# Batch 0 of a fused attention and feed-forward kernel: low parts of q and k of two head pairs, and the fourth pair's planes, on other engines

## The chip, the cores and the metric

The kernel runs on one core of a Trainium2 chip. The metric is the device time of one execution in microseconds; the median of the runs is compared. The engines are TensorE (PE, with its weight loads as PEld), VectorE (DVE), ScalarE (ACT), GpSimd (POOL) and SyncE (SP), which here only issues DMAs. Each engine works through its own queue in order and waits on semaphores that the others raise.

## The reference

Two parts follow each other. The first is attention over 8 batches of 8 heads, with 512 local and 32 global tokens of 64 dimensions; local queries see the global tokens and a window of 32 to each side. The second is a feed-forward part on the result, with a gate by a cosine.

```python
k_all = concat([k_g, k_l]); v_all = concat([v_g, v_l])
out_g = softmax(scale * q_g @ k_all.T) @ v_all
s_ll = where(abs(pos_q - pos_k) <= 32, scale * q_l @ k_l.T, -1e9)
s_lg = scale * q_l @ k_g.T
out_l = softmax(concat([s_lg, s_ll])) @ v_all
x = concat([out_g, out_l]) -> [4352 tokens, 512]
h = x @ w_in            # 512 -> 2048
out = (h * cos(h)) @ w_out   # 2048 -> 512
```

## The kernel before

**Precision.** The matmuls run on f16 operands. To keep float32 accuracy, each operand is first scaled by a power of two and split into a high part (its f16 rounding) and a low part (the rest, again f16). Three products high·high, high·low and low·high are summed in PSUM. So each value passes two steps: something writes the high part (a cast or a scaled copy), and a subtraction writes the low part. These splits are the bulk of the work of ACT, DVE and POOL.

**Attention, by pairs.** Heads are worked on in pairs, four to a batch; p is the pair, b the batch.
- `load_qk` (L452) loads q and k of a pair. For batch 0 the pairs 1 to 3 go into parts of the tile `wo_l`, which is not yet used for weights; the profile therefore calls them `wo_l`.
- `qk_a` to `qk_c` (L489 to L519) find the scale. `qk_a` needs the absolute sum from ACT (L495).
- `qk_d` (L521) makes the high part `qa` and the low part `kl`, 2 x 608 = 1216 columns. The list `QE0` (L76) gives the way for each pair of batch 0. 1: ACT scales in place (L237 in `scaled`), ACT casts (L533), POOL subtracts in four pieces of 304 columns (L231 in `pool_tt`). 2: the same, but POOL does the scaling (L240). 4: ACT scales and casts in one instruction (L537), DVE subtracts in one instruction that scales too (L538). Batch 1 on uses the last way.
- `qk_e` (L543) moves halves between partitions: two copies to `kh` (L547, L548), one from `kl` to the upper half of `qa` (L550), then one within `kl` (L552). For pair 0 of batch 0 some of them are made by DVE, otherwise by SP's DMAs. Each waits for the one whose source it overwrites.
- `sc_a`, `sc_b`, `sc_c` (L600 to L640) do scores (PE), mask and minimum (DVE, L623), and Exp (ACT, L446). A pair has four windows i of 192, 224, 224 and 192 columns, and two heads in each.
- `sc_d` (L672) normalizes the exponentials by the reciprocals `sm` and splits them into `planes`. The list `PLS` (L69) gives the way for each window in batch 0. 3: POOL multiplies (two instructions, L685), ACT casts (L693), POOL subtracts (two, L695). 4: ACT multiplies (L688), then the same cast and subtractions. 1: ACT writes the high part scaled (two, L702), DVE subtracts (two, L705). 2: as 1, but DVE writes the high part too (L704).
- `sc_e` (L707) transposes the planes; in batch 0 by PE (L714) with copies out of PSUM by ACT or DVE (L715).
- `av_a`, `av_b` (L729 to L778) multiply with v and write x, again as high and low part. `g_a` to `g_g` do the same for the global queries, once in two pairs.

**Weights.** W_in is decoded from 64-bit words in eight pieces (`w_in_piece`, L343): ACT scales (L237), DVE puts the bits together (L263, L266, L268), ACT casts the high part `wi_h` (L281), POOL subtracts `wi_l` (L231, four instructions of 256 columns). W_out is first read for its maxima (L407, DVE L288), then loaded again and decoded in 16 pieces during the first slots of the chunk loop; two of these loads, L244, use buffers that the W_in pieces hold before.

**Feed-forward.** The 4096 local tokens form 16 chunks of 256; a last one holds the 256 global tokens. A chunk has eight slots; in each, `m1_a` (L919) does 24 matmuls of W_in, then come range reduction and sine (L941, L942, L446), the gate (L954 to L961), and, three slots later, `m2_a` (L975 to L977) with W_out. Each chunk of batch 0 needs all four pairs of batch 0.

**Order.** The body lists each step with a slot and a phase (`at`), from slot -24 to the end; slots below 0 are the head. For batch 0, pair p starts at slot -21 + p and its steps follow at fixed distances (`tight`). Slot and phase give a priority. A planner with a timeline of its own then puts the instructions on the engines' queues: it takes the ready instruction with the best priority, by its own costs. So the order on a queue can change wherever an instruction moves to another engine.

Of the kernel before, what the change touches and what calls it, by code (L numbers as in the profile page):

```python
# [49 lines left out]
PL = 1  # L50
# [10 lines left out]
PL0 = 0  # L61
PL1 = 3
# [3 lines left out]
GFB = 3  # L66
GFW = 3
UW = 1
PLS = [3, 4, 3, 4]  # L69
DEFN = [0, 0]  # L70
TPE = [1, 1, 1, 1]
TPV = [1, 0, 1, 0]
WLV = 0
HIE = [1, 1, 1, 1]
SHV = [1, 0, 0, 0]
QE0 = [1, 4, 2, 1]  # L76
DI = 3
LVK = -1
LQK = -1
# [58 lines left out]
def body(tc, qk, v, wi, wo, mask, out):  # L138
# [5 lines left out]
    with ExitStack() as ctx:  # L144
# [376 lines left out]
        def qk_d(b, p):  # L521
# [6 lines left out]
            else:  # L528
                kl = ap_.tile([P, 2, NZ], F16, tag="kl", name=f"kl_{nm}")
            qe = QE[min(b, 2)] if b else QE0[p]  # L530
            if qe < 3:
# [110 lines left out]
        def sc_r(b, p):  # L642
            rr = st["sm", b, p]
            if b < 2 and DEFN[b]:
                nc.vector.tensor_scalar(rr, rr, 1e-9 * 2.0**14, 2.0**-22, op0=ALU.add, op1=ALU.mult)
                nc.vector.reciprocal(rr, rr)
                rh = ap_.tile([P, 8], F16, tag="rh", name=f"rh_{b}_{p}")
                rl = ap_.tile([P, 8], F16, tag="rl", name=f"rl_{b}_{p}")
                nc.vector.tensor_copy(rh, rr)
                nc.vector.tensor_tensor(rl, rr, rh, op=ALU.subtract)  # L650

                pr = ps.tile(
                    [P, SL], F32, tag="att" if b else "po", name=f"pr_{b}_{p}", bufs=3 if b else 2
                )
                for i in range(4):
                    for k, part in enumerate((rh, rl)):
                        for h in range(2):
                            r = part[:, 2 * i + h : 2 * i + h + 1]
                            r = bass.AP(tensor=r.tensor, offset=r.offset, ap=[r.ap[0], (0, D)])
                            nc.tensor.matmul(  # L660
                                pr[64 * h : 64 * h + 64, i * P : (i + 1) * P], r, ident16,
                                start=(i == 0 and k == 0), stop=(i == 3 and k == 1),
                                skip_group_check=True,
                            )
                sr = w1.tile([P, SL], F32, tag="sr", name=f"sr_{b}_{p}", bufs=1)
                nc.scalar.copy(sr, pr)
                st["sr", b, p] = sr
                return
            nc.vector.tensor_scalar(rr, rr, 1e-9, 2.0**-10, op0=ALU.add, op1=ALU.mult)
            nc.vector.reciprocal(rr, rr)  # L670

        def sc_d(b, p, i):  # L672
            if i == 0:
                sc_r(b, p)
            t, rr = st.pop(("t", b, p, i))[0], st["sm", b, p]
            w = WIN[i][1]
            pl = PLS[i] if b == 0 else (PL0, PL1, PL)[min(b, 2)]
            if b < 2 and DEFN[b]:
                pl = 5
            if pl in (0, 3, 4, 5):  # L680
                if pl == 3:
                    r = rr[:, 2 * i : 2 * i + 2]
                    rb = bass.AP(tensor=r.tensor, offset=r.offset, ap=[r.ap[0], (1, 2), (0, w)])
                    for h in range(2):
                        nc.gpsimd.tensor_tensor(t[:, h], t[:, h], rb[:, h], op=ALU.mult)  # L685
                if pl == 4:
                    for h in range(2):
                        nc.scalar.activation(t[:, h], t[:, h], AF.Copy, scale=rr[:, 2 * i + h : 2 * i + h + 1])  # L688
                for h in range(2 if pl == 0 else 0):
                    nc.vector.tensor_scalar(t[:, h], t[:, h], rr[:, 2 * i + h : 2 * i + h + 1], None, op0=ALU.mult)  # L690
                hi = planes[i][:, :, 0, OFF[i] : OFF[i] + w]
                lo = planes[i][:, :, 1, OFF[i] : OFF[i] + w]
                (nc.scalar.copy if pl != 5 or HIE[i] else nc.vector.tensor_copy)(hi, t)  # L693
                for h in range(2):
                    nc.gpsimd.tensor_tensor(lo[:, h], t[:, h], hi[:, h], op=ALU.subtract)  # L695
            else:
                for h in range(2):
                    hi = planes[i][:, h, 0, OFF[i] : OFF[i] + w]
                    lo = planes[i][:, h, 1, OFF[i] : OFF[i] + w]
                    r = rr[:, 2 * i + h : 2 * i + h + 1]  # L700
                    if pl == 1:
                        nc.scalar.activation(hi, t[:, h], AF.Identity, scale=r)  # L702
                    else:
                        nc.vector.tensor_scalar(hi, t[:, h], r, None, op0=ALU.mult)  # L704
                    nc.vector.scalar_tensor_tensor(lo, t[:, h], r, hi, op0=ALU.mult, op1=ALU.subtract)  # L705
# [308 lines left out]
        def attn_pair(b, p, o):  # L1014
# [11 lines left out]
            for i in range(4):  # L1026
                at(o["sc"][i], PA, sc_a, b, p, i)
                at(o["sc"][i], PA if o["tight"] else PC, sc_b, b, p, i)
                at(o["ex"], PI, sc_c, b, p, i)
                at(o["sd"], PF, sc_d, b, p, i)  # L1030
                at(o["tr"][i], PA2, sc_e, b, p, i)
# [177 lines left out]
```

## Time and profile before

| | us |
|---|---|
| median of 3 runs | 1044.99 (1041.33 to 1047.4) |
| profiled execution, device time | 1047.05 |
| its span, first to last instruction | 1045.2 |
| busy in the span: PE, DVE, ACT, POOL | 891.6, 705.4, 720.4, 475.4 |
| mean granted TensorE clock | 0.957 |

A table of stretches gives, for each, its start and end, its length, the busy time of PE, PEld, DVE, ACT and POOL with the number of instructions, the granted clock, the DMA share and GB/s. A timeline lists instructions by start and duration in us; in square brackets stands the idle time before an instruction and who ended it. Neighbouring instructions of one kind are merged (x4). The chain of waits goes back from the last instruction of a stretch, at each step to what released it. A group row has busy us, mean ns, and idle time before.

### The profile page before, as it was taken

What the parts mean: (1) busy time and instruction counts of PE and PEld (TensorE: products, weight loads), DVE (VectorE), ACT (ScalarE), POOL (GpSimd) and SP (SyncE); (2) the same over time, 40 slices, a digit from 0 to 9 for tenths busy, and PEclk for the clock granted to TensorE, in tenths of its full rate; (3) what the DMA queues carried; (4) which work ended last, traced back from release to release, by engine and by line L of the source; (5) the groups of instructions that cost most, each with busy time, mean ns of one, the idle gap of its engine ahead of it and who ended that gap; (6) DMA issues with size and microseconds to landing.
All of it is one profiled execution on the core that took longest, in us unless ns stands there. A gap on an engine that the chain in (4) does not pass through costs nothing.

```text
span 1045.2 us, 21138 instructions
## 1 busy us (share of the span) xinstructions
PE 891.6 (85%) x7947; PEld 608.2 (58%) x7947; DVE 705.4 (67%) x1801; ACT 720.4 (69%) x1470; POOL 475.4 (45%) x513
## 2 busy tenths in 40 slices
PE   1344677678999998999899988999889999999996
PEld 0232554454566665666666655666656676666663
DVE  5996588887468777777778677777777776433231
ACT  5786788887477776877687777867777777444342
POOL 3698477886333332433243423333334333444442
PEclk9995898887999999999999999999999999999998
DMA  9786025867254546353554455355545452200000
GB/s 371 274 299 222 14 69 147 201 150 159 93 109 92 117 90 146 86 114 89 152 100 117 95 147 106 94 104 141 107 104 102 109 89 57 48 21 21 1 21 21
DMA packets 165823, 120.20 MB, mean 115 GB/s; under 512 B 143064, under 2 KB 143064, under 8 KB 163672
## 3 DMA queue, kind: packets, MB, share of 16 engines
q1 hardware_dynamic: 165720, 118.85, 45.2%
q8 instruction: 62, 1.02, 0.4%
q14 instruction: 41, 0.34, 0.1%
HBM read 56.00 MB, written 8.91 MB: 62 GB/s over the span
## 4 chain that ended last, share of the span: by engine, by line
PE 36%; DVE 22%; ACT 15%; DMA 13%; POOL 7%; issue 5%; SPq 1%; ACTq 0%; DVEq 0%; POOLq 0%
PE ph L919 15%; DMA qkr<-qk 7%; PE po L975 6%; PE po L977 5%; PE po L976 5%; DVE planes L705 4%; DVE t L623 3%; DMA vr<-v 3%; ACT planes L702 3%; ACT L446 3%; DVE u L942 3%; ACT t L446 2%; POOL planes L695 2%; PE acc L750 2%; DVE kl L538 2%
## 5 line engine op out<-in xcount | busy, mean ns | idle before, releaser
L919 PE MATMUL ph<-xh,wi_h 128*128 128x256 f16 x1024 | 282.8, 277 | 17.1 <-DVE gf L956 15.2
L919 PE MATMUL ph<-xl,wi_h 128*128 128x256 f16 x1024 | 283.1, 277 | 0.0
L919 PE MATMUL ph<-xh,wi_l 128*128 128x256 f16 x1024 | 282.9, 276 | 0.0
L961 POOL TENSOR_TENSOR gl<-gf,gh 128x512 f16<-128x512 f32 x136 | 167.3, 1234 | 236.7 <-ACT gh L960 236.6
L954 POOL TENSOR_TENSOR w<-w 128x512 f32<-128x512 f32 x136 | 142.4, 1051 | 268.8 <-ACT w L446 268.8
L919 PEld LDWEIGHTS <-wi_h 128*128 128x128 f16 x2176 | 212.2, 99 | 60.7 <-issue 18.6
L975 PE MATMUL po<-wo_h,gh 128*128 128x512 f16 x544 | 206.5, 384 | 29.1 <-DVE o L983 17.9
L976 PE MATMUL po<-wo_l,gh 128*128 128x512 f16 x544 | 208.2, 383 | 7.3 <-POOL wo_l L231 7.2
L977 PE MATMUL po<-wo_h,gl 128*128 128x512 f16 x544 | 207.8, 383 | 0.0
L446 ACT ACTIVATE w<-u,ca 128x512 f32<-128x512 f32 x136 | 97.7, 721 | 109.5 <-DVE u L942 107.6
L942 DVE SCALAR_TENSOR_TENSOR u<-u,cm,ph 128x512 f32<-128x512 f32 x136 | 100.8, 741 | 97.4 <-ACT u L941 97.4
L446 ACT ACTIVATE t<-t,mn 128x192 f32<-128x192 f32 (+1 forms) x256 | 116.9, 458 | 49.7 <-DVE mn L623 49.1
L956 DVE SCALAR_TENSOR_TENSOR gf<-w,ph 128x512 f32<-128x512 f32 x136 | 92.6, 681 | 56.3 <-POOL w L954 56.1
L960 ACT CAST gh<-gf 128x512 f16<-128x512 f32 x136 | 83.1, 611 | 68.3 <-DVE gf L956 59.5
L919 PEld LDWEIGHTS <-wi_l 128*128 128x128 f16 x1088 | 107.9, 99 | 15.1 <-issue 1.2
L941 ACT ACTIVATE u<-ph,cm 128x512 f32<-128x512 f32 x136 | 92.2, 679 | 21.5 <-PE ph L919 20.0
L623 DVE CUSTOM_DVE_ANT_0 t<-ps,msk,al 128x192 f32<-128x192 f32 (+1 forms) x256 | 99.2, 425 | 11.3 <-PE ps L607 11.1
L977 PEld LDWEIGHTS <-gl 128*128 128x128 f16 x544 | 53.6, 99 | 71.7 <-issue 9.9
L976 PEld LDWEIGHTS <-gh 128*128 128x128 f16 x544 | 53.5, 98 | 70.1 <-issue 21.8
L705 DVE SCALAR_TENSOR_TENSOR planes<-t,sm,planes 128x192 f16<-128x192 f32 (+1 forms) x192 | 83.9, 486 | 10.5 <-ACT planes L702 10.4
L975 PEld LDWEIGHTS <-gh 128*128 128x128 f16 x544 | 53.2, 98 | 62.3 <-issue 13.9
L446 ACT ACT_TABLE_LOAD x57 | 73.1, 1283 | 1.0
(188 smaller groups left out, 1435.7 us busy)
## 6 DMA issues: line engine op xcount, KB each, us to landing
qkr<-qk SPq DMA_DIRECT2D x29, 608.0 KB, 4.4
vr<-v SPq DMA_DIRECT2D x8, 1280.0 KB, 8.4
kh<-qa SPq DMA_DIRECT2D x62, 152.0 KB, 2.6
out<-o SPq DMA_DIRECT2D x34, 256.0 KB, 3.1
raw_wm<-wo SPq DMA_DIRECT2D x16, 512.0 KB, 6.5
qa<-kl SPq DMA_DIRECT2D x31, 152.0 KB, 3.4
kl<-kl SPq DMA_DIRECT2D x31, 152.0 KB, 3.6
wo_h<-wi SPq DMA_DIRECT2D x4, 1024.0 KB, 9.1
```

The lines of the kernel that those rows point to most:

```text
L446: ins = nc.scalar.activation(*a, **k).ins
L623: nc.vector.tensor_tensor_reduce(t[:, h], pt[:, h], msk[:, MOFF[i] : MOFF[i] + w], al, 3.0e38, ALU.add, ALU.min, mn[:, h : h + 1],)
L705: nc.vector.scalar_tensor_tensor(lo, t[:, h], r, hi, op0=ALU.mult, op1=ALU.subtract)
L919: nc.tensor.matmul(ph[:, a], w[:, kc, f], x[:, kc, q], start=first and ip == 0, stop=last and ip == 2, skip_group_check=True,)
L941: nc.scalar.activation(u, ph, AF.Identity, bias=m)
L942: nc.vector.scalar_tensor_tensor(u, u, m, ph, op0=ALU.subtract, op1=ALU.subtract)
L954: nc.gpsimd.tensor_tensor(w, w, w, op=ALU.mult)
L956: nc.vector.scalar_tensor_tensor(gf, w, 0.5, st.pop(("ph", c, j)).rearrange("p a b -> p (a b)"), op0=ALU.subtract, op1=ALU.mult,)
L961: nc.gpsimd.tensor_tensor(gl, gf, gh, op=ALU.subtract)
L975: nc.tensor.matmul(po[k], gh[:, q], wo_h[:, f], start=(f == 0), stop=False)
L976: nc.tensor.matmul(po[k], gh[:, q], wo_l[:, f], start=False, stop=False)
L977: nc.tensor.matmul(po[k], gl[:, q], wo_h[:, f], start=False, stop=(f == NJ - 1))
```

## The change

Two lists are changed and one line reads them.
- `QE0`: pairs 2 and 3 of batch 0 go from ways 2 and 1 to way 4.
- `PLS` gets a row for each pair. Pairs 0 to 2 keep ways 3, 4, 3, 4 for the four windows. Pair 3 gets 1, 2, 1, 4: windows 0 and 2 by ACT (high part) and DVE (low part), window 1 by DVE alone, window 3 as before.

```diff
-PLS = [3, 4, 3, 4]
+PLS = [[3, 4, 3, 4], [3, 4, 3, 4], [3, 4, 3, 4], [1, 2, 1, 4]]
...
-QE0 = [1, 4, 2, 1]
+QE0 = [1, 4, 4, 4]
...
-            pl = PLS[i] if b == 0 else (PL0, PL1, PL)[min(b, 2)]
+            pl = PLS[p][i] if b == 0 else (PL0, PL1, PL)[min(b, 2)]
```

## The prediction

> **What bounds the kernel now.** I read the table of stretches first, since the edit touches only batch 0. PE, PEld, DVE, ACT and POOL busy, granted clock, DMA share and GB/s for each stretch:
>
> ```profile
> 0.00:60.00 60.00, 13.18 (x85) 8.87 (x85) 46.91 (x135) 40.88 (x83) 34.42 (x52) 1.00 0.85 322
> 60.00:122.00 62.00, 32.84 (x380) 23.87 (x381) 40.85 (x117) 42.66 (x87) 47.27 (x70) 0.75 0.54 180
> 122.00:190.00 68.00, 51.62 (x424) 36.74 (x422) 53.62 (x135) 60.86 (x115) 49.34 (x67) 0.90 0.41 110
> 190.00:260.00 70.00, 51.34 (x523) 33.40 (x523) 59.11 (x158) 55.50 (x117) 53.45 (x70) 0.83 0.75 166
> 260.00:500.00 240.00, 230.49 (x2060) 156.19 (x2058) 169.01 (x437) 169.98 (x354) 88.17 (x77) 0.99 0.48 107
> ```
>
> From 260 us on PE is busy 96% of the time (230.49 of 240). Before 122 us it is busy 46.0 of 122 us: this is the head, in which batch 0 is prepared and PE waits for other engines. Only here can the edit gain. Cutting the head finer shows who holds it:
>
> ```profile
> 48.80:75.00 26.20, 10.92 (x100) 8.08 (x98) 25.86 (x59) 20.10 (x28) 26.15 (x30) 1.00 0.89 295
> 75.00:91.50 16.50, 4.44 (x62) 3.19 (x59) 16.15 (x54) 12.73 (x31) 16.50 (x25) 0.72 0.98 360
> 91.50:101.00 9.50, 6.50 (x63) 5.12 (x65) 1.39 (x3) 4.04 (x6) 9.22 (x16) 0.50 0.23 74
> ```
>
> Three things are full at once from 48.8 to 91.5 us: POOL (42.65 of 42.7 us), DVE (42.01) and, from 75 us, the DMA engines (0.98). After 91.5 us only POOL stays full (9.22 of 9.5) while DVE falls to 1.39: POOL is the last to finish. The chain of waits, followed back from the end of the head (start, duration, what), says the same:
>
> ```profile
> 48.85 4.53 POOL wi_l L231 x4
> 55.51 2.57 POOL t L685 x4
> 64.34 6.66 POOL planes L695 x7
> 74.68 9.75 DMA kh<-qa
> 88.31 3.05 POOL t L685 x4
> 91.35 3.21 POOL planes L695 x6
> 94.56 2.52 POOL wi_l L231 x4
> 97.11 0.33 SPq L244
> 97.53 4.23 DMA kl<-kl
> ```
>
> The last steps matter most. SP's queue holds a load of raw W_out (L244) until POOL has finished wi_l at 97.08, because the buffer is still in use. Behind it stands the copy kl<-kl of the fourth pair (97.53), and that pair's scores cannot start until it lands at 101.76. So the fourth pair, and with it the first full chunk of the feed-forward part, starts when POOL's queue has run to that wi_l.
>
> **The change part by part.** POOL's timeline has the work that goes:
>
> ```profile
> 53.34 2.21 POOL L240 TENSOR_TENSOR wo_l<-wo_l,qs 128x1216 f32<-128x1216 f32 x1
> 61.42 2.93 POOL L231 TENSOR_TENSOR kl<-wo_l,qa 128x304 f16<-128x304 f32 x4
> 79.26 3.09 POOL L231 TENSOR_TENSOR kl<-wo_l,qa 128x304 f16<-128x304 f32 x4
> 108.88 2.01 POOL L685 TENSOR_TENSOR t<-t,sm 128x192 f32<-128x192 f32 x4 [8.15 <-DVE sm L670]
> 111.57 4.54 POOL L695 TENSOR_TENSOR planes<-t,planes 128x192 f16<-128x192 f32 x8 [0.69 <-ACT planes L693]
> ```
>
> *Edit A, q and k of the third and fourth pair.* POOL loses 2.21 + 2.93 + 3.09 = 8.23 us, all ahead of the wi_l that releases L244. ACT: for the third pair a cast becomes a scaled activation; for the fourth, one of two activations goes. DVE gains two subtractions of 1216 columns. What those cost and how such an operation acts on POOL is in these rows (group summary: min/median/max ns):
>
> ```profile
> L538 DVE SCALAR_TENSOR_TENSOR kl<-qkr,qs,qa x28: 1466/1696/2345, 141.1 to 835.8; 128x1216 f16<-128x1216 f32 x28
> L231 POOL TENSOR_TENSOR wi_l<-y_wi,wi_h x32: 664/670/1698, 40.4 to 100.0; 128x256 f16<-128x256 f32 x32
> 51.63 1.22 DVE L268 SCALAR_TENSOR_TENSOR y_wi<-y_wi,lo_wi 128x1024 uint32<-128x1024 uint32 x1
> 51.68 1.70 POOL L231 TENSOR_TENSOR wi_l<-y_wi,wi_h 128x256 f16<-128x256 f32 x1
> ```
>
> The same POOL subtraction takes 0.67 us normally and 1.70 us when it starts just behind a DVE operation with two inputs in SBUF: it lost 1.03 us to an operation of 1.22 us, 0.84 of its length. The two new DVE operations are of this kind. At 1.70 us each (the median, since POOL is busy beside them), DVE gains 3.4 us; POOL loses 0.84 x 1.47 = 1.2 us to each, 2.5 in all (the undisturbed length, as the extra is DVE waiting for POOL). So POOL's queue gets shorter by 8.23 - 2.5 = 5.7 us.
>
> The Trainium skill, "SBUF — State Buffer", section "Who interferes with whom", says that a DVE instruction with two SBUF inputs and a GpSimd instruction that reads SBUF exclude each other, so that the loser waits for the whole instruction. By that rule edit A would be worth a little less, an estimated 5.3 us, and moving work between these two engines pays only by the difference of their speeds; the row above agrees with the exclusion and puts the loss at 1.03 of 1.22 us.
>
> The bounds of A. Upper: no blocking, 8.2 us. Lower: DVE, itself full, holds the queue. The DVE step that feeds the decisive wi_l is this one:
>
> ```profile
> 86.48 1.34 DVE L268 SCALAR_TENSOR_TENSOR y_wi<-y_wi,lo_wi 128x1024 uint32<-128x1024 uint32 x1
> 89.91 1.04 ACT L281 CAST wi_h<-y_wi 128x1024 f16<-128x1024 f32 x1
> 94.53 2.55 POOL L231 TENSOR_TENSOR wi_l<-y_wi,wi_h 128x256 f16<-128x256 f32 x4
> ```
>
> With DVE's order unchanged and 3.4 us more in front, it ends at 91.2; plus 1.04 for the cast and 2.55 for POOL that is 94.8, against 97.08 now: 2.3 us gained. In between is the likeliest, nearer POOL's side, because 10.6 us of DVE's work in this stretch are the maxima of W_out, needed only after the scores of batch 0, and the planner may put these behind:
>
> ```profile
> L288 DVE TENSOR_REDUCE wos<-raw_wm 128x1 f32<-128x512 f32 x16 | 10.6, 673 | 0.0
> ```
>
> I take 5.7.
>
> *Edit B, planes of the fourth pair.* POOL loses 10 operations after 108.88: four multiplications (2.01 us) and six of eight subtractions; it now ends at 116.11. ACT loses the multiplications and cast of the second window and the casts of the first and third, and gets four scaled activations instead. DVE gets two scaled copies and six subtractions. Batch 2 on does this, and its rows price the subtraction and the activation; a scaled copy by DVE (L704) appears nowhere, so I bound it between the 0.2 us of the reciprocal on 8 columns and the 0.478 us of the subtraction, and take the latter, the same width:
>
> ```profile
> L705 DVE SCALAR_TENSOR_TENSOR planes<-t,sm,planes 128x192 f16<-128x192 f32 (+1 forms) x64 | 27.6, 478 | 3.0 <-ACT planes L702 3.0
> L702 ACT ACTIVATE planes<-t,sm 128x192 f16<-128x192 f32 (+1 forms) x64 | 24.3, 452 | 0.0
> 108.53 0.20 DVE L670 RECIPROCAL sm<-sm 128x8 f32<-128x8 f32 x1
> 111.13 0.78 DVE L835 SCALAR_TENSOR_TENSOR planes_g<-gt,gsm,planes_g 128x544 f16<-128x544 f32 x1 [1.72 <-ACT planes_g L834]
> ```
>
> DVE starts at 108.73 and needs 8 x 0.478 = 3.8 us, plus 0.78 for planes_g: done at 113.3. ACT has four activations of 0.45, planes_g and the fourth window, about 4 us, in parallel. That is 2.8 us before POOL's 116.11. But PE was already at the transposes in this time:
>
> ```profile
> 111.55 3.87 PE L714 MATMUL tr<-ident,planes 128*128 128x128 f16 x26 [5.76 <-ACT planes L693]
> ```
>
> Of 32 transposes 26 were done by 115.42, so part of the 2.8 us can be lost to PE and the copies out of PSUM: 0 to 2.8, and I take 2.0. The cover is there, since DVE is nearly idle just before (1.39 of 9.5 us); without it DVE's 3.8 us would lie on the path.
>
> *Sum.* 5.7 + 2.0 = 7.7 us off the head. After it nothing has a time of its own: DMA is at 0.41 from 122 to 190 us, and PE, ACT and DVE follow the slots of the chunk loop, so the whole rest moves forward. The profiled execution took 1047.05 us (span 1045.2 plus 1.85 around it): 1039.4. It lay 2.1 us above the median of the runs, 1044.99, against which the same saving gives **1037.3 us**. With the bounds (2.3 to 11.0 us) the forecast's own range is 1034.0 to 1042.7.
>
> **The rivals.** *The fourth pair overtakes.* Its low part no longer stands behind the planes of the second pair and the vl in POOL's queue (79.26). Also its qa needs no scaled copy before it: in ACT's queue that was at 63.66, the cast only at 68.50.
>
> ```profile
> 63.66 1.32 ACT L237 ACTIVATE wo_l<-wo_l,qs 128x1216 f32<-128x1216 f32 x1
> 68.50 1.20 ACT L533 CAST qa<-wo_l 128x1216 f16<-128x1216 f32 x1
> kh<-qa SPq DMA_DIRECT2D x62, 152.0 KB, 2.6
> ```
>
> With qa at 64.97 the copies to kh could leave at about 66 instead of 74.68, ahead of the bulk loads that made the one at 74.68 last 9.75 us instead of the usual 2.6, and kl<-kl ahead of L244. That is up to 8.7 us for the earlier issue, half of the 7.1 that the copy can get shorter, and B's 2.0: 14.3 us, about 1030.7. Against it: SP's order is the planner's, and scores, planes and wi_l still need DVE and POOL, both full.
>
> *The gain is swallowed.* Fourth pair and chunk loop compete from 122 to 190 us, where ACT is busy 60.86 of 68 us; or the saturated DMA (0.98), not POOL, sets when kh, qa and kl of the fourth pair land, and A shrinks to about nothing. Then B alone or less is left: 0 to 3 us, about 1043.5.
>
> *DVE becomes the bound (slower).* DVE has no idle time to speak of from 48.8 to 91.5 us, and takes 3.4 us from A there and 3.8 from B. It decides if the planner leaves the maxima in front, and a new operation also makes DVE stand still, waiting for ACT's qa (cast now at 68.50) with y_wi and the scores of the third pair queued behind it. On DVE's path with unchanged order 2.3 us are gained (above), so from a standstill of 2.3 us on the head grows. If DVE's whole added work, 3.4 + 3.8 us, comes out on the path, that is 7.2 us: 1052.2. The spread of L538 (1466 to 2345 ns) shows that such an operation can take still longer. For it: two engines equally full. Against it: after 91.5 us DVE has 8.1 of 9.5 us free, so it need not be last.
>
> **How the numbers follow.** Forecast 0.50, overtaking 0.12, swallowed 0.20, DVE 0.18. 0.5% of the time is 5.2 us, about what a measurement of this kernel can tell from no change. Faster by more: 0.82 of the forecast (gains spread as a triangle from 2.3 to 11.0 with its peak at 7.7 have 0.18 below 5.2) plus overtaking, 0.53. Within: 0.18 of the forecast, 0.85 of swallowed and 0.2 of DVE, 0.29. Slower: the rest, 0.18. The range reaches from 1027, taking in the overtaking case with 3 us of scatter (the runs lie between 1041.33 and 1047.4), to 1049, the swallowed case with the same and half of the DVE case.
>
> **What would show it.** Right: POOL's queue full from 48.8 to only about 95 us; L244 and kl<-kl of the fourth pair issued near 91 to 92 instead of 97; the last subtraction of batch 0's planes near 108 instead of 116.11; beyond 260 us the same PE share. The subtractions on POOL that run beside the new kl of DVE should take up to 1.9 us. Wrong: DVE with gaps in front of kl, waiting for qa; the decisive y_wi later than 86.48; kh<-qa still 9.75 us long and L244 no longer in front of kl<-kl; or a head shorter by 5 us and more, with a longer stretch from there to x of batch 1.

## The result, and the profile after

| | us |
|---|---|
| before, median of 4 runs | 1044.88 (1041.33 to 1047.4) |
| after, median of 4 runs | 1034.22 (1030.87 to 1036.3) |
| ratio after to before | 0.9897, 95% interval 0.9858 to 0.9937 |
| spans of the two profiled executions | 1045.2 and 1032.6 |

The change makes the kernel 1.0% faster, 10.8 us by the ratio (6.6 to 14.8). The forecast was 7.7 us less, with a range of 2.3 to 11.0. The measured middle lies above that and close to the upper end, but 7.7 is still inside the measured interval.

The table of stretches of the kernel after, with the same cuts and columns as before:

```profile
0.00:60.00 60.00, 13.58 (x87) 9.02 (x87) 46.14 (x133) 41.33 (x84) 33.62 (x53) 1.00 0.87 321
60.00:122.00 62.00, 38.23 (x493) 29.64 (x494) 53.66 (x148) 50.10 (x102) 40.91 (x57) 0.83 0.60 186
122.00:190.00 68.00, 53.14 (x392) 36.78 (x391) 54.06 (x145) 60.26 (x118) 53.21 (x73) 0.85 0.49 127
...
48.80:75.00 26.20, 12.92 (x109) 9.52 (x109) 26.05 (x63) 20.07 (x30) 24.47 (x29) 1.00 0.98 306
75.00:91.50 16.50, 5.99 (x68) 4.19 (x68) 16.26 (x52) 13.56 (x30) 13.59 (x22) 0.56 1.02 378
91.50:101.00 9.50, 7.77 (x80) 6.31 (x78) 8.50 (x36) 9.25 (x28) 6.03 (x11) 0.68 0.28 102
```

From 60 to 122 us all engines but POOL do more in the same time: PE 38.23 instead of 32.84 us, DVE 53.66 instead of 40.85. POOL, full from 48.8 to 101 us before (51.87 us), is busy 44.09 us there and has gaps:

```profile
66.45 11.01 POOL L594 TENSOR_TENSOR vl<-vr,vh 128x256 f16<-128x256 f32 x12 [0.91 <-ACT vh L592]
85.87 2.89 POOL L231 TENSOR_TENSOR wi_l<-y_wi,wi_h 128x256 f16<-128x256 f32 x4 [2.91 <-ACT wi_h L281]
88.71 2.00 POOL L685 TENSOR_TENSOR t<-t,sm 128x192 f32<-128x192 f32 x4
90.68 2.56 POOL L231 TENSOR_TENSOR wi_l<-y_wi,wi_h 128x256 f16<-128x256 f32 x4
93.19 4.34 POOL L695 TENSOR_TENSOR planes<-t,planes 128x224 f16<-128x224 f32 x8
104.96 1.06 POOL L695 TENSOR_TENSOR planes<-t,planes 128x192 f16<-128x192 f32 x2 [7.43 <-ACT planes L693]
```

In its idle times POOL now waits for ACT's casts. Partly because of them its work of this stretch ends only 3.2 us earlier (97.53 instead of 100.72). The wi_l that releases L244 ends 8.3 us earlier (88.76 instead of 97.08): the planner also put it ahead of the third pair's multiplications (L685) and planes, most of which ran ahead of it before. DVE is still full up to 91.5 us and does not drop afterwards (8.50 instead of 1.39): what had waited behind POOL now comes earlier. The head's end can be read off ACT's first scaling of raw W_out for the chunk loop. Timeline of ACT, before and then after:

```profile
122.53 0.74 ACT L237 ACTIVATE y_wo<-wo_h,wsc 128x512 f32<-128x512 f32 x1
```

```profile
112.42 0.75 ACT L237 ACTIVATE y_wo<-wo_h,wsc 128x512 f32<-128x512 f32 x1
```

10.1 us of the saving is there by then. SP's queue after shows how the fourth pair gets there (kh and kl copies from 66.52 on, the held load of raw W_out), with the landing times of the two copies kl<-kl of that stretch below:

```profile
66.52 0.55 SPq L547 DMA_DIRECT2D kh<-qa  x1
71.13 0.47 SPq L550 DMA_DIRECT2D qa<-kl  x1
77.45 0.48 SPq L552 DMA_DIRECT2D kl<-kl  x1
88.78 4.80 SPq L244 DMA_DIRECT2D raw_wo<-wo  x2
...
DMA to landing us min/median/max: 3.9/7.5/11.1
```

The fourth pair's copies start 8.2 us earlier (66.52 instead of 74.68), and kl<-kl no longer stands behind L244: it leaves at 77.45 instead of 97.53. But it takes 11.1 us in the stretch where DMA is busy all the time, and PE starts on the pair's products with kl at 88.55 (101.81 before), 13.3 us earlier. The chain of waits after, from its middle to the fourth pair's planes, has become one of DVE:

```profile
71.86 1.55 DVE y_wi L268
83.62 1.10 DVE y_wi L268
87.30 1.54 ACT t L688 x4
90.72 2.52 POOL wi_l L231 x4
93.23 2.16 POOL planes L695 x4
99.83 0.58 DVE planes L704 x2
```

In the chain of before, POOL held most of the long pieces from 48.85 to 97.1; here its first long piece comes at 90.72, and up to 86.35 it is DVE's operations, one after the other.

### The profile page after: what moved, and what is told of

The parts are those of the page before. It is cut to its first block, busy times and chain, and to the rows that moved or that the text cites. A ratio compares the mean times of both kernels' runs of the same rounds, so it can differ in the third digit from the quotient of the medians.

```text
span 1032.6 us, 21117 instructions
## 1 busy us (share of the span) xinstructions
PE 893.3 (87%) x7947; PEld 609.2 (59%) x7947; DVE 710.7 (69%) x1811; ACT 717.9 (70%) x1468; POOL 461.8 (45%) x494
## 4 chain that ended last, share of the span: by engine, by line
PE 33%; DVE 28%; ACT 15%; DMA 11%; POOL 5%; issue 5%; SPq 1%; ACTq 0%; DVEq 0%; POOLq 0%
PE ph L919 13%; DMA qkr<-qk 7%; PE po L975 5%; PE po L976 5%; PE po L977 5%; DVE planes L705 4%; DVE t L623 4%; DVE u L942 3%; ACT L446 3%; ACT planes L702 3%; ACT t L446 3%; DMA vr<-v 2%; DVE kl L538 2%; POOL w L954 2%; DVE qm L497 2%
## 5 line engine op out<-in xcount | busy, mean ns | idle before, releaser
L623 DVE CUSTOM_DVE_ANT_0 t<-ps,msk,al 128x192 f32<-128x192 f32 (+1 forms) x256 | 99.5, 426 | 11.7 <-PE ps L607 11.2
L705 DVE SCALAR_TENSOR_TENSOR planes<-t,sm,planes 128x224 f16<-128x224 f32 (+1 forms) x198 | 88.6, 496 | 10.7 <-ACT planes L702 10.7
L702 ACT ACTIVATE planes<-t,sm 128x192 f16<-128x192 f32 (+1 forms) x196 | 74.3, 453 | 0.0
```

Source lines behind the costliest of these rows:

```text
L623: nc.vector.tensor_tensor_reduce(t[:, h], pt[:, h], msk[:, MOFF[i] : MOFF[i] + w], al, 3.0e38, ALU.add, ALU.min, mn[:, h : h + 1],)
```

## The experiments

Three theories: (1) POOL's queue is too long in the head, and what leaves it is gained; (2) the fourth pair overtakes, because its low part and its copies no longer wait for POOL; (3) DVE is the bound, so that the gain would be small or turn round. All ratios are against the kernel before, run beside each; us are worked out from the ratio and about 1046.5 us.

### The two edits apart

Edit A alone (`PLS[3]` as in the other pairs):

```diff
-PLS = [..., [1, 2, 1, 4]]
+PLS = [..., [3, 4, 3, 4]]
```

> Edit A alone (low parts of q and k of the third and fourth pair by DVE; the fourth pair's planes as in the kernel before). Theory 1, length of POOL's queue: 8.2 us leave it, so the run is about 8 us faster than before. Theory 2, the fourth pair overtakes (its copies leave SP early because its low part no longer stands in POOL's queue): also about 8 us. Theory 3, DVE as the bound: at most 2 us. The first scaling of W_out by ACT, which marks the end of the head (122.53 us before, 112.42 after), comes at about 114.5 by theories 1 and 2, at 120 or later by theory 3.

Measured: 0.9895 (0.9870 to 0.9920), 11.0 us faster (8.4 to 13.6). Its end of the head, from ACT's timeline:

```profile
114.04 0.74 ACT L237 ACTIVATE y_wo<-wo_h,wsc 128x512 f32<-128x512 f32 x1
```

That is 8.5 us earlier than before, as theories 1 and 2 expect. Edit A is nearly the whole change.

Edit B alone (the new `PLS`):

```diff
-QE0 = [1, 4, 4, 4]
+QE0 = [1, 4, 2, 1]
```

> Edit B alone (the fourth pair's planes; q and k as before). Prediction's price: 2.0 us faster, between 0 and 2.8; the last subtraction of batch 0's planes on POOL ends near 113 instead of 116.11 us. If the two edits help each other (POOL free when the fourth pair comes), less than 2 us; if the ring of PSUM buffers for the transposes holds it, 0.

Measured: 0.9984 (0.9969 to 0.9999), 1.7 us faster (0.1 to 3.2). POOL's timeline:

```profile
113.57 1.06 POOL L695 TENSOR_TENSOR planes<-t,planes 128x192 f16<-128x192 f32 x2 [12.59 <-issue]
```

The last subtraction ends at 114.63, 1.5 us earlier than before, where 3 us (near 113) were expected; the time agrees with the price of 2.0 us. On top of edit A nothing of B is to be seen: A alone has the ratio 0.9895, both together 0.9897. The intervals leave room for the 1.7 us.

### The two pairs apart

```diff
-QE0 = [1, 4, 4, 4]
+QE0 = [1, 4, 4, 1]     # third pair only
+QE0 = [1, 4, 2, 4]     # fourth pair only
```

Both have `PLS` as before.

> Only the third pair's q and k on the new way (POOL loses 2.21 + 2.93 us); fourth pair and planes as before. Theory 1, length of POOL's queue: 5.1 us less one block of 1.2, so 4 us faster. Theory 2, overtaking: the fourth pair's low part still stands in POOL's queue, only some 5 us earlier; 0 to 2 us faster. Theory 3, DVE: up to 2 us slower.

> Only the fourth pair's q and k on the new way (POOL loses 3.09 us, ACT one pass of 1.3); third pair and planes as before. Theory 1, length of POOL's queue: 3.1 us less one block of 1.2, so 2 us faster. Theory 2, overtaking: its copies to kh leave SP near 66 instead of 74.68 us and its copy of kl ahead of the held load of raw W_out; most of edit A's gain, 6 to 8 us. Theory 3, DVE: up to 2 us slower.

Measured: third pair 0.9958 (0.9938 to 0.9977), 4.4 us; fourth pair 0.9972 (0.9953 to 0.9990), 2.9 us. The sizes fit theory 1 (4 and 2 expected), not theory 2, which put 6 to 8 us on the fourth pair and at most 2 on the third. The fourth pair's copies did overtake, so its 2.9 us can also come from the order of the copies, which by itself gave about as much (below). SP's queue with the fourth pair alone:

```profile
67.47 0.55 SPq L547 DMA_DIRECT2D kh<-qa  x1
...
87.67 0.48 SPq L552 DMA_DIRECT2D kl<-kl  x1
93.36 3.85 SPq L244 DMA_DIRECT2D raw_wo<-wo  x2
```

kh left 7.2 us earlier and kl<-kl 9.9 us earlier, ahead of L244, and only 2.9 us came of it: kl landed 6.4 us later, at 94.1, but PE had transposes of the third pair, which wait for POOL's planes, in front of the fourth pair's first matmuls with kl (98.37). The halves add up to 7.3 us, less than the 11.0 of both; the intervals overlap, so that this is only pointed to.

### Is it POOL's time or the order of the copies?

The changed kernel with POOL's queue filled up again:

```diff
+            if b == 0 and p > 1:
+                for k in range(7 if p == 2 else 4):
+                    ...  # x: a new tile; c: half of the columns
+                    nc.gpsimd.tensor_tensor(x, t[:, k // 2 % 2, c], qa[:, k // 2 % 2, c], op=ALU.subtract)
```

> The changed kernel with 11 further POOL subtractions of 304 columns (about 8.2 us) on the same inputs, right after qa of the third and fourth pair, into a tile that nobody reads. So POOL's queue is as long as before, while kl of both pairs still comes from DVE. Theory 1, length of POOL's queue: nearly all of edit A's gain is lost, the run is 7 to 9 us slower than the changed kernel, about 2 us faster than before. Theory 2, what counts is when and in which order kl of the third and fourth pair comes: less than 3 us slower than the changed kernel.

Measured: 1.0008 (0.9988 to 1.0028): the whole gain was gone, also B's. But the experiment held more than it was to hold: the added work took 10.5 us, and SP's copies qa<-kl waited for the added work, which reads what they overwrite, and the fourth pair's kl<-kl left only at 98.24. So it was repeated with added work on the half of qa that no copy overwrites:

```diff
+                    ...  # loop and tile x as above
+                    y = qa[0:64, k // 2 % 2, 304 * (k % 2) : 304 * (k % 2) + 304]
+                    nc.gpsimd.tensor_tensor(x[0:64], y, y, op=ALU.subtract)
```

> As the run with POOL refilled, but the 11 added POOL subtractions read only the lower half of qa, which no copy overwrites, so that no DMA waits for them: POOL's queue is long again, and only that. In the run before, the copies qa<-kl (SP) waited for the added work too. Theory 1, length of POOL's queue: at least 6 of the 8.2 us come back as time, the run is near before. Theory 2, the copies of the third and fourth pair had waited for POOL: the gain mostly stays, less than 3 us slower than the changed kernel.

Measured: 1.0023 (1.0002 to 1.0045); the added work took 8.4 us. SP's queue and, below, DVE's timeline of this run:

```profile
67.42 0.55 SPq L552 DMA_DIRECT2D kh<-qa  x1
...
78.14 0.48 SPq L557 DMA_DIRECT2D kl<-kl  x1
...
96.03 3.84 SPq L244 DMA_DIRECT2D raw_wo<-wo  x2
```

```profile
91.83 0.52 DVE L364 TENSOR_SCALAR xs<-pw_i,wr_i 128x4 f32<-128x4 f32 x1
92.27 3.15 DVE L365 TENSOR_SCALAR xs<-pw_i,wr_i 128x4 f32<-128x4 f32 x1
...
96.82 2.73 DVE L389 TENSOR_SCALAR xs<-xs,gam 128x4 f32<-128x4 f32 x1
...
100.93 0.51 DVE L820 CUSTOM_DVE_ANT_0 gt<-gps,zero,gal 128x288 f32<-128x288 f32 x1
```

Below them the table of stretches from 91.5 us on, and the first scaling of raw W_out in ACT's timeline:

```profile
91.50:101.00 9.50, 2.63 (x23) 1.43 (x24) 9.29 (x20) 4.71 (x10) 9.50 (x16) 0.50 0.28 88
```

```profile
125.43 0.74 ACT L237 ACTIVATE y_wo<-wo_h,wsc 128x512 f32<-128x512 f32 x1
```

(Lines behind the added ones lie five further here.) The copies leave as early as in the changed kernel (kl<-kl 78.14 against 77.45) and L244 stands behind them. Still nothing is left of the gain, and the head ends 2.9 us later than in the kernel before (125.43 against 122.53). So theory 2 does not carry the gain: early copies brought nothing in this run, where POOL is full again. POOL was busy without a gap from 91.5 to 101 us (9.50 of 9.5), and two DVE operations on four columns took 3.15 and 2.73 us beside it. PE began the fourth pair's products with kl at 94.29, behind transposes of the third pair that waited for planes, and DVE took up the scores only at 100.93 (91.18 in the changed kernel).

The run is not POOL's time alone: the planner's order differs too. In the changed kernel the products with kl stand ahead of those transposes on PE, and the wi_l that releases L244 ahead of the third pair's last multiplications on POOL.

### Does DVE's added work cost anything?

The kernel before with 8 more DVE subtractions of 304 columns for the two pairs, results unused:

```diff
+            if b == 0 and p > 1:
+                for k in range(4):
+                    ...  # x: a new tile; c: half of the columns
+                    nc.vector.scalar_tensor_tensor(x, t[:, k // 2, c], s, qa[:, k // 2, c], op0=ALU.mult, op1=ALU.subtract)
```

> The kernel before with four more DVE subtractions of 304 columns with two inputs in SBUF for each of the third and fourth pair (8 in all, about 3.2 us), whose result nobody reads; POOL keeps its work. It is the cost side of edit A by itself. The prediction's price: POOL is blocked for 0.84 of their length, 2.5 to 2.7 us slower than before. DVE as the bound: 3.2 us slower, more if DVE has to wait for qa. No cost at all (both hidden): 0.

Measured: 0.9989 (0.9972 to 1.0006), between 2.9 us faster and 0.6 slower. The eight operations took 6.5 us (819 ns each on average), twice what was expected. The head did get longer:

```profile
125.09 0.74 ACT L237 ACTIVATE y_wo<-wo_h,wsc 128x512 f32<-128x512 f32 x1
```

125.09 against 122.53 is 2.6 us, about the predicted price, but no loss at the end was measured. So theory 3 falls for this size; the stretch behind the head seems to take up such a delay.

The opposite, the changed kernel with DVE relieved: the maxima of W_out over half of the columns.

```diff
-                o, raw.bitcast(F32)[:, 1::2], axis=AX.X, op=ALU.max, apply_absolute_value=True
+                o, raw.bitcast(F32)[:, 1 : n : 2], axis=AX.X, op=ALU.max, apply_absolute_value=True
...
-            maxes["wo", j] = raw_max(wos[:, j : j + 1], raw)
+            maxes["wo", j] = raw_max(wos[:, j : j + 1], raw, 512)
```

> The changed kernel with the 16 maxima of W_out (L288) taken over half of the columns: DVE has some 16 x 0.27 = 4.3 us less work in the head, loads are the same. What is left out: the second half of W_out's columns in the search for its largest value. If DVE is the bound of the head now: 3 to 4 us faster than the changed kernel. If the DMA engines are: within 1 us.

Measured: 0.9899 (0.9872 to 0.9926), the same as the changed kernel's 0.9897. The head ended 1.6 us earlier, again without an effect on the end:

```profile
110.81 0.74 ACT L237 ACTIVATE y_wo<-wo_h,wsc 128x512 f32<-128x512 f32 x1
```

DVE fills the chain of waits in the head, but 4.3 us less of it (16 maxima of 0.41 instead of 0.67 us) brought no measurable gain.

### L244 and the loads

The kernel before, and the one with the third pair alone, each with an ordering line added (cut here to that line), which puts L244 behind the fourth pair's kl<-kl in SP's queue:

```diff
+            tc.add_manual_dep(ld.ins, st["klc", 0, 3].name, order, reason="copy_first")
```

> The kernel before with one order more in SP's queue: the two held loads of raw W_out (L244) stand behind the fourth pair's copy kl<-kl instead of ahead of it. No work changes. If L244 held the fourth pair, as the prediction says: kl<-kl leaves at about 92.6 us (qa<-kl landed) instead of 97.53, the fourth pair's scores and the head are 4 to 5 us earlier and the run 4 us faster. If the third pair's planes in POOL's queue held it anyway: 0 to 1 us.

> The third pair's q and k on the new way (edit A's first half) and the same order in SP's queue: L244 behind the fourth pair's kl<-kl. If edit A's two halves gave 11 us together but 7.3 one by one because L244 stayed in front in the first half: the run is 7 us or more faster than before. If the fourth pair's low part itself has to leave POOL: as with the first half alone, 4 to 5 us faster.

Measured: 0.9969 (0.9952 to 0.9987) for the first, 3.2 us faster (1.4 to 5.0) without any work changed; 0.9949 (0.9927 to 0.9972) for the second, 5.3 us, not clearly more than the third pair alone (4.4). SP's queue of the first:

```profile
86.25 0.48 SPq L551 DMA_DIRECT2D qa<-kl  x1
92.68 0.47 SPq L553 DMA_DIRECT2D kl<-kl  x1
97.27 3.98 SPq L244 DMA_DIRECT2D raw_wo<-wo  x2
```

kl<-kl leaves at 92.68, as expected to a tenth; the head ends 2.0 us earlier (120.52), less than the 4 to 5 expected. So L244 did hold the fourth pair, with POOL as full as before, and the change takes this hold away as well as POOL's time. Which share of the change's gain that is stays open: the changed kernel with L244 put back ahead of kl<-kl was not run.

The loads of raw W_out listed two slots later in the changed kernel:

```diff
-WOL = -5
+WOL = -3
```

> The changed kernel with the eight loads of raw W_out (L416) listed two slots later. In the changed kernel these stand in SP's queue just ahead of the fourth pair's copy kl<-kl, which takes 11.1 us in the stretch where the DMA engines are busy all the time. If the DMA engines now set the fourth pair: kl lands 5 us or more earlier and the run is 2 to 5 us faster than the changed kernel. If DVE sets it (the chain of waits in the head is mostly DVE's): no change within 1.5 us.

Measured: 0.9886 (0.9861 to 0.9911), the same as the changed kernel. It tells nothing: the planner left the loads ahead of kl<-kl (now at 78.02), which again took 11.2 us. What a shorter copy would bring stays open.

### One step further

The third pair's first window on ACT and DVE as well:

```diff
-PLS = [..., [3, 4, 3, 4], [1, 2, 1, 4]]
+PLS = [..., [1, 4, 3, 4], [1, 2, 1, 4]]
```

> The changed kernel with the third pair's first window split by ACT and DVE too: POOL loses four more operations (about 2.4 us) in the head, DVE gets two subtractions (0.95 us). If POOL's queue is still what the head waits for (its planes of the third pair end at 97.53): 1 to 2 us faster than the changed kernel. If DVE or the DMA engines are the bound, or the stretch behind the head takes it back: within 1 us.

Measured: 0.9890 (0.9863 to 0.9917), the same, with 1.7 us less of POOL's time from 48.8 to 101 us (42.38 against 44.09). No version tried is clearly faster than the changed kernel.

## Why the prediction was right, and where it was off

- *POOL bounds the head.* Right: with POOL filled again the whole gain was gone, twice, the second time with the copies as early as in the changed kernel. The second run's changed order on PE and POOL and its long DVE operations can belong to the loss, too.
- *Edit A, 5.7 us between 2.3 and 8.2.* That POOL's work was worth removing was right, the size too small: A alone gave 11.0 us (8.4 to 13.6), above the upper bound of 8.2, with 8.5 in the head of the trace. Two things were missed. First, the blocking of POOL by the new kl. By itself it came as priced. DVE's and POOL's timelines of the kernel after show one POOL subtraction beside each new kl:

```profile
58.92 1.93 DVE L538 SCALAR_TENSOR_TENSOR kl<-wo_l,qs,qa 128x1216 f16<-128x1216 f32 x1
59.53 1.73 POOL L695 TENSOR_TENSOR planes<-t,planes 128x192 f16<-128x192 f32 x1
67.38 1.82 DVE L538 SCALAR_TENSOR_TENSOR kl<-wo_l,qs,qa 128x1216 f16<-128x1216 f32 x1
67.89 1.85 POOL L594 TENSOR_TENSOR vl<-vr,vh 128x256 f16<-128x256 f32 x1
```

  Undisturbed these take 0.54 and 0.66 us, so POOL lost 1.2 us to each, as forecast. But it lost less to other DVE operations: the 60 operations that stay with POOL from 48.8 to 101 us took 43.64 us before (51.87 less the 8.23 removed) and 44.09 after. The net loss was 0.45 us, not 2.5. Second, L244 was treated as something that moves along with POOL; in fact the planner put kl<-kl ahead of it. In the kernel before, this order by itself is worth 3.2 us; beside the third pair's half it gave 0.9 more, within the noise. The planner also changed the order on POOL, so how the 11.0 us split between less work and other orders stays open.
- *The price of kl on DVE, 1.70 us.* They took 1.93 and 1.82. The cover that the prediction counted on, DVE's free time from 91.5 to 101 us, is used up in the changed kernel (8.50 of 9.5 us busy); even so, halving the maxima of W_out changed nothing at the end.
- *Edit B, 2.0 us between 0 and 2.8.* Measured 1.7 alone, and nothing visible on top of A. So the sum 5.7 + 2.0 erred in both terms, in opposite directions. That the total of 10.8 still lies just inside the upper end of 11.0 is in part luck.
- *"The whole rest moves forward."* Right for 10 us, not for 2: 2.6 us more of head (DVE's added work) and 1.6 less (half maxima) were not seen at the end.
- *Overtaking, 0.12.* It did happen, kh at 66.52 as worked out (66) and kl<-kl ahead of L244. It was wrong to keep it apart from the forecast: the same edit does both, and what was measured is a mixture of the two. Its 14.3 us were too much. The copy to kh did get shorter, 4.0 instead of 9.75 us from issue to landing; but kl<-kl, which the sum left alone, took 11.1 instead of 4.23. And with POOL refilled early copies brought nothing.
- *Swallowed, 0.20.* Not so: the end came 10.8 us earlier, about as much as the head (10.1).
- *DVE as the bound, 0.18.* Not so: 6.5 us of added work cost at most 0.6 us.
- *What was to be seen.* The POOL subtractions beside the new kl take 1.73 and 1.85 us (up to 1.9 forecast). The last subtraction of batch 0's planes ends at 106.02 (108 forecast). L244 left at 88.78, kl<-kl at 77.45 (91 to 92 forecast for both). POOL's queue is not full until 95: it has 3.8 us of gaps before, and its work of this stretch ends at 97.5. From 260 to 500 us PE is busy 229.98 us, before 230.49.

How the loss of the run with POOL full splits into POOL's own time, the time that DVE lost beside it and the changed order stays open; filling POOL without touching the others was not tried.

## What to carry to other kernels

Where two engines are equally full, ask which of them still has work when the other runs dry: here that one held the stretch, and moving work off it paid although the other full engine got it. An in-order DMA queue adds its own hold: look what stands in front of the late copy and whether an edit lets the planner reorder the two. Price such a hold by itself; here one ordering line gave 3.2 us with no work moved.

## What the runs showed of the hardware

The length of a small DVE operation beside a full POOL was not expected. In the run with added work on half of qa, the operation of L365 on four columns took 3.15 us (92.27 to 95.42); it takes 0.80 in the kernel before and 0.65 in the one after. POOL's timeline beside it:

```profile
92.81 0.69 POOL L543 TENSOR_TENSOR x<-qa 64x304 f16<-64x304 f16 x1
93.46 2.54 POOL L231 TENSOR_TENSOR wi_l<-y_wi,wi_h 128x256 f16<-128x256 f32 x4
```

None of these POOL operations lasts longer than 0.69 us, and four of them began and ended while DVE's one was open, without idle time between them. The Trainium skill, "SBUF — State Buffer", section "Who interferes with whom", says that when a DVE instruction in a two-port mode meets GpSimd, the one that issues first holds the shared ports for its whole instruction, and the other waits. No run shows in which mode DVE's operation ran. Its length fits a wait for POOL, but one that did not end with an operation of POOL, only after several. A full POOL alone does not make it so: in the kernel before POOL had no gap either when L365 ran (81.6 us), and it took 0.80. The long form was seen in one profiled execution, and its cause is not shown.
